# Decode scratch moved to PSUM, an order that knows the SBUF turn between VectorE and GpSimd, and first loads in another order

## The chip, the cores and the metric

The kernel runs on one core of a Trainium2 chip. The metric is the device time of one execution in microseconds (us). Five engines work side by side, each through its own instruction stream in order: TensorE (PE) multiplies into PSUM, ScalarE (ACT) and VectorE (DVE) compute on SBUF and PSUM, GpSimd (POOL) on SBUF, and SyncE (SP) issues most of the transfers.

## The reference

Attention over pooled keys, then a dense layer pair:

```python
k_p = k.reshape(B, H, Sp, 8, D).mean(axis=3)       # B=8, H=8, S=576, D=64, Sp=72
v_p = v.reshape(B, H, Sp, 8, D).mean(axis=3)
attn = softmax(q @ k_p.T / sqrt(D))                # 576 x 72 per head
x = (attn @ v_p) as 4608 x 512
h = x @ w_in                                       # 512 x 2048
out = (h * sigmoid(1.702 * h)) @ w_out             # 2048 x 512
```

`w_in` and `w_out` arrive as float64, so the kernel has to make fp32 numbers out of 64-bit words itself. All large products are done as three products of a high and a low part.

## The kernel before

Tokens go through the dense layers in nine chunks of 512: chunk c is 512 of the 576 tokens of batch c, the last chunk gathers the 64 left over of all eight. For each of 16 slices f of 128 hidden columns, PE makes h (L893 to L895), ACT makes the gelu twice, once rounded (gh, L908) and once in full (g, L914), DVE or POOL makes the low part gl = g - gh (L918), and PE adds gh and gl times w_out to o (L934 to L936). Chunk 0 is done in two halves of 256 tokens and pairs of slices, since it runs while the weights still arrive.

Attention of a batch: `sum_keys` and `sum_values` pool k and v (for batches 0 and 1 by matmuls against the identity, tiles red_k, red_v), `scores` makes sps on PE and on DVE nm (the row maximum) and sc, exp on ACT, the sum sm, its reciprocal, then tail and main (L582), and `weigh` turns these on PE (tpt, apt), splits them on ACT and DVE (at, ah, al) and multiplies by v (pav); ACT and DVE write the high and low half of x (L723, L729). Batch 0 has two pieces (256 and 320 tokens).

Weights: 33 pieces of 512 or 256 columns, in order w_in slice, w_out slice, and so on. `decode` takes for each: ACT writes e = |high word| scaled (L833), ACT scales the low word in place (L840), DVE shifts e (L846), DVE merges it with the sign into raw (L853), POOL adds the low word (L860), ACT rounds to the high part of w (L867), and POOL or DVE makes the low part (L873). The scratch e lies in SBUF, in a ring of two buffers ("osb") that only the output copies use later.

The order of all of this comes from `Plan`: each task has an engine, a cost, a due time, the tasks before it, and the buffers of limited rings that it takes. `order()` runs a clock over the five engines, gives each free engine the ready task with the earliest due time for which its rings have room, and the instructions are then written in the order found. PSUM has a ring "h" of two banks (dense h tiles, the key and value sums of batch 0), "a" of two and "o" of four. A DVE task costs 1.3 times as much in the plan while POOL is busy, a POOL task 1.2 times while DVE is.

Of the kernel before, what the change touches and what calls it, by code (L numbers as in the profile page):

```python
# [9 lines left out]
F32 = mybir.dt.float32  # L10
# [7 lines left out]
P = 128  # L18
POOL = 8

ENGINES = ("DMA", "ACT", "DVE", "POOL", "PE")

# [24 lines left out]
class Task:  # L47
    __slots__ = "engine us emit due after before bufs ready left begun table k".split()


class Plan:
# [6 lines left out]
    def add(self, engine, us, emit, reads=(), writes=(), due=None, table=None, also=()):  # L58
        t = Task()
        t.engine, t.us, t.emit, t.table = engine, us, emit, table  # L60
# [54 lines left out]
    def order(self, log=None):  # L115
        free = dict.fromkeys(ENGINES, 0.0)
        free["DMA"] = 2.0
        ready = {e: [] for e in ENGINES}
        for t in self.tasks:
            if not t.left:  # L120
                ready[t.engine].append(t)
        now, running, table, placed = 0.0, [], None, []
        busy = {}
        while len(placed) < len(self.tasks) or running:
            for end, k, t in sorted(running):
# [7 lines left out]
                for o in t.after:  # L133
                    o.left -= 1
                    o.ready = max(o.ready, end + self.wait(t, o))
                    if not o.left:
                        ready[o.engine].append(o)
            for e in ENGINES:
                if free[e] > now + 1e-9:
                    continue  # L140
                best = None
                for t in ready[e]:
                    if t.ready <= now + 1e-9 and (best is None or (t.due, t.k) < (best.due, best.k)) and self.room(t):
                        best = t
                if best is None:
                    continue
                t = best
                ready[e].remove(t)
                us = t.us
                if t.table not in (None, table):  # L150
# [18 lines left out]
            times += [t.ready for e in ENGINES for t in ready[e] if t.ready > now + 1e-9]  # L169
            if not times:  # L170
                if len(placed) < len(self.tasks):
                    stuck = [(t.engine, t.due, [b.name for b in t.bufs if b.ring is not None and not b.held and not b.ring.room]) for e in ENGINES[1:] for t in ready[e]] + [b.name for b in {b for t in placed for b in t.bufs if b.users and b.ring is not None}]
                    raise RuntimeError(f"stuck at {now}: {stuck}")
# [6 lines left out]
def attention_moe_kernel(ctx: ExitStack, tc: tile.TileContext, q, k, v, w_in, w_out, out):  # L180
# [53 lines left out]
    def dve(n, emit, reads, writes, rate=1.0, due=None, also=()):  # L234
        return plan.add("DVE", 0.14 + n / 960.0 * rate, emit, reads, writes, due, also=also)

    def pool(n, emit, reads, writes, rate=2.4, due=None):
        return plan.add("POOL", 0.06 + n * rate * 1e-3, emit, reads, writes, due)
# [95 lines left out]
    def spread(b, raw, bd, u, nm):  # L334
# [14 lines left out]
        else:  # L349
# [21 lines left out]
            [(bd, u)],  # L371
        )
# [4 lines left out]
    def sum_keys(b, m):  # L377
# [3 lines left out]
        for u in range(NU):  # L381
# [23 lines left out]
                [(m.tbd, u)],  # L405
            )
# [27 lines left out]
    def sum_values(b, m):  # L434
# [11 lines left out]
        def tsrc():  # L446
# [7 lines left out]
            [m.vl],  # L454
        )
# [7 lines left out]
            [m.vt],  # L463
        )
# [4 lines left out]
    def scores(b, piece, m, whole_q=None):  # L469
# [74 lines left out]
        for ns, g in groups:  # L544
# [26 lines left out]
            dve(200, inverse, [], [(sm, ns)])  # L571


        if b < TURNED:
            main = buf(att, [P, NT, H, KM], F32, "main", f"main{n}")
            tail = buf(att, [P, NT, H, KT], F32, "tail", f"tail{n}")
            for dst, cols in ((tail, slice(KM, KEYS)), (main, slice(0, KM))):
                for ns, g in groups:
# [10 lines left out]
                        [(dst, ns)],  # L589
                    )  # L590
# [3 lines left out]
        for i in range(4):  # L594
# [3 lines left out]
            for u in range(NU):  # L598
# [11 lines left out]
                    rate=1.8,  # L610
                )
            for r in range(4):
# [11 lines left out]
                    rate=1.25,  # L624
# [3 lines left out]
    def weigh(b, piece, m, main, tail):  # L628
# [29 lines left out]
        for u in range(NU):  # L658
# [16 lines left out]
            dve(npc, lo, [pt], [at])  # L675
# [3 lines left out]
        for j in range(NJ):  # L679
# [10 lines left out]
            else:  # L690
# [16 lines left out]
                [al],  # L707
            )
# [42 lines left out]
    def gather_left(c):  # L751
# [8 lines left out]
        for j in range(NJ):  # L760
# [12 lines left out]
                [(x, (1, 0, j))],  # L773
            )
# [36 lines left out]
    def decode(i):  # L811
# [4 lines left out]
        e = buf(moe, [P, DM], F32, "osb", f"e{i}")  # L816
# [7 lines left out]
        def eu():  # L824
# [24 lines left out]
            rate=0.5,  # L849
# [229 lines left out]
```

## Time and profile before

| what | value |
|---|---|
| median of 3 runs | 977.33 us (976.6 to 977.58) |
| the profiled execution | 976.99 us, its span 975.2 us |
| PE busy | 933.1 us (96%) |
| DVE, ACT, POOL busy | 551.7, 394.0, 246.7 us |
| mean granted clock of PE | 0.978 |

The span is the time from the first to the last instruction. PE is busy in 100 of 100 us between 200 and 300 us; the first 150 us, in which the weights arrive and are decoded and the first two batches go through attention, look different:

```profile
PE   5688899999999999999999999999999999999996
DVE  2899986688737793679457945794588210000000
PEclk8689999999999999999999999999999999999998
DMA  8982232330133012401240124002200020001001
```

Each digit is a slice of 24.4 us, in tenths; PEclk is the granted clock of PE.

### The profile page before, as it was taken

The numbers are of one execution on the slowest core, as the hardware profiler recorded it, in microseconds if no ns is written. First come the engines' busy times: TensorE is split into PE (matmuls) and PEld (weight loads), VectorE is DVE, ScalarE is ACT, GpSimd is POOL, SyncE is SP. The second block draws the span as 40 slices with busy tenths as digits, with TensorE's granted clock in tenths as the row PEclk, the third lists the DMA queues.
The fourth block names the chain that finished last, engine by engine and source line by source line (L and its number), as shares of the span: only waits on it lengthen the run. The fifth ranks groups of instructions, "written<-read, shape, count | busy, mean of one in ns | idle before, by whom it ended". The sixth has DMA issues, their size and how long they took to land.

```text
span 975.2 us, 12254 instructions
## 1 busy us (share of the span) xinstructions
PE 933.1 (96%) x4470; PEld 771.5 (79%) x4470; DVE 551.7 (57%) x1038; ACT 394.0 (40%) x745; POOL 246.7 (25%) x196
## 2 busy tenths in 40 slices
PE   5688899999999999999999999999999999999996
PEld 5467788888888888888888888888888878887884
DVE  2899986688737793679457945794588210000000
ACT  2777774444334432443244334343434231222112
POOL 1447841121222122212221221122221222222221
PEclk8689999999999999999999999999999999999998
DMA  8982232330133012401240124002200020001001
GB/s 199 348 300 50 54 61 71 92 75 12 36 79 81 12 30 68 99 12 25 68 104 11 28 65 103 11 23 71 70 1 1 6 87 1 1 0 44 1 1 43
DMA packets 104875, 59.52 MB, mean 61 GB/s; under 512 B 79472, under 2 KB 87664, under 8 KB 104688
## 3 DMA queue, kind: packets, MB, share of 16 engines
q1 hardware_dynamic: 99568, 49.31, 20.1%
q10 hardware_dynamic: 5248, 9.44, 2.8%
q8 instruction: 35, 0.57, 0.2%
q14 instruction: 24, 0.20, 0.1%
HBM read 48.23 MB, written 10.49 MB: 60 GB/s over the span
## 4 chain that ended last, share of the span: by engine, by line
PE 85%; DVE 6%; issue 2%; DMA 2%; ACT 2%; SPq 1%; ACTq 1%; POOL 0%; POOLq 0%; DVEq 0%
PE h L893 13%; PE o L934 13%; PE h L894 13%; PE h L895 13%; PE o L935 12%; PE o L936 12%; PE sps L509 4%; DVE raw L853 2%; DVE e L846 1%; PE pav L714 1%; PE pav L716 1%; PE pav L717 1%; PE pav L715 1%; DMA raw<-in_moe_w_in_dram 1%; SPq L289 1%
## 5 line engine op out<-in xcount | busy, mean ns | idle before, releaser
L918 POOL TENSOR_TENSOR gl<-g,gh 128x512 fp32r<-128x512 f32 x132 | 172.8, 1309 | 644.3 <-ACT g L914 522.3
L893 PE MATMUL h<-x,w 128*128 128x512 f32 (+1 forms) x640 | 241.9, 378 | 1.8 <-ACT g L914 1.8
L894 PE MATMUL h<-x,w 128*128 128x512 f32 (+1 forms) x640 | 237.2, 371 | 0.0
L895 PE MATMUL h<-x,w 128*128 128x512 f32 (+1 forms) x640 | 237.0, 370 | 0.0
L934 PE MATMUL o<-w,gh 128*128 128x512 f32 x576 | 229.4, 398 | 1.2 <-ACT gh L908 0.7
L936 PE MATMUL o<-w,gl 128*128 128x512 f32 x576 | 226.2, 393 | 2.5 <-DVE gl L918 1.4
L935 PE MATMUL o<-w,gh 128*128 128x512 f32 x576 | 227.3, 395 | 0.0
L908 ACT ACTIVATE gh<-h 128x512 fp32r<-128x512 f32 x144 | 86.1, 598 | 303.0 <-PE h L895 270.9
L893 PEld LDWEIGHTS h<-x,w 128*128 128x128 f32 x640 | 121.9, 190 | 24.3 <-ACT g L914 2.7
L895 PEld LDWEIGHTS h<-x,w 128*128 128x128 f32 x640 | 121.8, 190 | 20.5
L894 PEld LDWEIGHTS h<-x,w 128*128 128x128 f32 x640 | 122.0, 191 | 18.6
L936 PEld LDWEIGHTS o<-w,gl 128*128 128x128 f32 x576 | 108.5, 188 | 28.4 <-DVE gl L918 2.6
L934 PEld LDWEIGHTS o<-w,gh 128*128 128x128 f32 x576 | 108.5, 188 | 27.2 <-issue 2.4
L935 PEld LDWEIGHTS o<-w,gh 128*128 128x128 f32 x576 | 108.7, 189 | 20.6
L616 DVE TENSOR_TENSOR main<-sc,sm 32x256 f32<-32x256 f32 (+1 forms) x192 | 115.8, 603 | 2.8
L914 ACT ACTIVATE g<-h 128x512 f32<-128x512 f32 x144 | 85.4, 593 | 25.5 <-PE h L895 20.6
L498 DVE STREAM_TRANSPOSE qt<-qr 128x256 f32<-128x256 f32 (+1 forms) x56 | 25.8, 467 | 57.5 <-PE sps L509 55.8
L509 PE MATMUL sps<-k,qt 128*128 128x144 f32 (+1 forms) x320 | 55.5, 302 | 0.6 <-DVE at L667 0.6
L509 PEld LDWEIGHTS sps<-k,qt 128*128 128x128 f32 (+1 forms) x320 | 45.3, 185 | 10.4 <-issue 2.0
L860 POOL TENSOR_TENSOR raw<-raw 128x512 uint32<-128x512 uint32 x30 | 35.1, 1169 | 59.5 <-DVE raw L853 48.1
L723 ACT CAST x<-pav 128x256 fp32r<-128x256 f32 x64 | 23.7, 371 | 46.6 <-PE pav L717 45.6
L527 DVE TENSOR_REDUCE nm<-sps 128x4 f32<-128x288 f32 x96 | 37.1, 387 | 6.6 <-PE sps L509 6.4
(89 smaller groups left out, 878.1 us busy)
## 6 DMA issues: line engine op xcount, KB each, us to landing
out_dram<-osb ACTq DMA_DIRECT2D x32, 256.0 KB
raw<-in_moe_w_in_dram SPq DMA_DIRECT2D x15, 512.0 KB
raw<-in_moe_w_out_dram SPq DMA_DIRECT2D x15, 512.0 KB
kv_False<-in_k_dram SPq DMA_DIRECT2D x28, 256.0 KB
kv_True<-in_v_dram SPq DMA_DIRECT2D x28, 256.0 KB
qr<-in_q_dram SPq DMA_DIRECT2D x112, 40.0 KB
qr<-in_q_dram SPq DMA_DIRECT2D x112, 32.0 KB
tl<-in_v_dram SPq DMA_DIRECT2D x48, 64.0 KB
```

The costliest lines, as they stand in the source:

```text
L509: nc.tensor.matmul(ps()[:ns, t * PW : (t + 1) * PW], lhsT=qt()[:, s0 - o0 : s0 - o0 + ns], rhs=m.k2()[:, j], start=True, stop=True,)
L527: lambda ns=ns, g=g, hs=hs, view=view: nc.vector.tensor_reduce(out=nm()[:ns, g, hs], in_=view(), axis=AX.X, op=ALU.max, negate=True),
L616: lambda r=r, a=a, half=half, rows=rows, cols=cols, nt=nt: nc.vector.tensor_tensor(out=main()[32 * r : 32 * (r + 1), :, cols].rearrange("p ...
L893: nc.tensor.matmul(o, lhsT=w[:, 0, j], rhs=xs[:, 0, j], start=j == 0, stop=False)
L894: nc.tensor.matmul(o, lhsT=w[:, 1, j], rhs=xs[:, 0, j], start=False, stop=False)
L895: nc.tensor.matmul(o, lhsT=w[:, 0, j], rhs=xs[:, 1, j], start=False, stop=j == NJ - 1)
L908: lambda: nc.scalar.activation(out=gh(), in_=h(), func=AF.Gelu_apprx_sigmoid),
L914: 512, lambda: nc.scalar.activation(out=g(), in_=h(), func=AF.Gelu_apprx_sigmoid), [h], [g], table="gelu"
L918: engine.tensor_tensor(out=gl(), in0=g(), in1=gh().bitcast(F32), op=ALU.subtract)
L934: nc.tensor.matmul(o, lhsT=gh()[:, i, tok], rhs=w[:, 0], start=f == 0, stop=False)
L935: nc.tensor.matmul(o, lhsT=gh()[:, i, tok], rhs=w[:, 1], start=False, stop=False)
L936: nc.tensor.matmul(o, lhsT=gl()[:, i, tok], rhs=w[:, 0], start=False, stop=f == NF - 1)
```

## The change

Four things change. The scratch e of the decode goes from SBUF to a PSUM bank of the ring "h", the ring of two that the dense h tiles use too. The plan no longer stretches DVE and POOL tasks by factors: tasks marked `port` (all POOL tasks, and most DVE tasks whose operands all lie in SBUF) exclude one another, the later one waits in the plan until the other is through, and a marked DVE task ranks 20 us later while POOL holds the port; some planned rates change with it. The low parts of the weights, and of chunk 0's gl, are POOL tasks that DVE may take instead once their due time has passed; before, every fourth piece and the first slices were fixed to DVE. And the first loads come in another order.

```diff
     def order(self):
+        port = {"DVE": 0.0, "POOL": 0.0}
...
+                rival = {"DVE": "POOL", "POOL": "DVE"}.get(e)
+                blocked = rival is not None and port[rival] > now
                 best = None
                 for t in ready[e]:
-                    if t.ready <= now + 1e-9 and (best is None or (t.due, t.k) < (best.due, best.k)) and self.room(t):
-                        best = t
+                    if t.ready > now + 1e-9 or e != t.engine and now < t.due:
+                        continue
+                    rank = (t.due + (BLOCKED if blocked and t.port and e == "DVE" else 0.0), t.k)
+                    if (best is None or rank < best[0]) and self.room(t):
+                        best = rank, t
...
-                if e == "DVE" and free["POOL"] > now:
-                    us *= 1.3
-                if e == "POOL" and free["DVE"] > now:
-                    us *= 1.2
+                if t.port:
+                    if blocked:
+                        us += port[rival] - now
+                    port[e] = now + us
...
-        us = nbytes / 1e3 / (340.0 if run >= 1024 else 160.0 if run >= 256 else 90.0)
+        us = nbytes / 1e3 / (340.0 if run >= 1024 else 110.0 if run >= 256 else 80.0)
...
-        e = buf(moe, [P, DM], F32, "osb", f"e{i}")
+        e = buf(ps_h, [P, DM], F32, "h", f"e{i}")
...
             lambda: nc.vector.tensor_scalar(out=eu(), in0=eu(), scalar1=3, scalar2=None, op0=ALU.logical_shift_left),
             [],
             [e],
-            rate=0.5,
...
-        if i % 4 != 2:
-            pool(n, lambda: lower(nc.gpsimd), [(rb, rk), (h, (0, c0))], [(h, (1, c0))])
-        else:
-            dve(n, lambda: lower(nc.vector), [(rb, rk), (h, (0, c0))], [(h, (1, c0))])
+        pool(
+            n,
+            lambda: lower(nc.gpsimd),
+            [(rb, rk), (h, (0, c0))],
+            [(h, (1, c0))],
+            other=lambda: lower(nc.vector),
+        )
...
-        if c == 0 and fs[0] < 12:
-            dve(512, lambda: rest(nc.vector), [g, gh], [gl])
-        else:
-            pool(512, lambda: rest(nc.gpsimd), [g, gh], [gl])
+        pool(512, lambda: rest(nc.gpsimd), [g, gh], [gl], other=(lambda: rest(nc.vector)) if c == 0 else None)
...
-        for n, what in enumerate("w k0 k1 tk tv q q v0 v1 w w w w w q w q w q".split()):
+        for n, what in enumerate("k0 k1 tk q q v0 v1 tv w w w w w q q q w w".split()):
```

In the last line w is a weight piece, k and v the main parts of batch 0, tk and tv its last keys and values (tile tl), q a tile of 128 queries. The line numbers below differ between the two kernels; after, L863 is the old L833, L870 the old L840, L876 and L882 the old L846 and L853, L896 the old L867.

PE's stream at the start of the program, before (numbers behind the names are running counts; red_v sums values, kps turns the keys, sps are scores):

```order
L412 MATMUL kps_0_151<-ident,kbd_143 128x2x64 x2
L415 MATMUL kps_0_151<-ident,tbd_145 128x4x8
L486 MATMUL qps_0_0_160<-ident,q_0_126 128x128 x2
L486 MATMUL qps_0_1_164<-ident,q_0_126 128x128 x2
L412 MATMUL kps_1_169<-ident,kbd_143 128x2x64 x2
L415 MATMUL kps_1_169<-ident,tbd_145 128x4x8
L344 MATMUL red_v_180<-kv_97,ident 128x128 x8
L509 MATMUL sps_0_0_194<-k_167,qt_0_0_176 128x144 x2
L509 MATMUL sps_0_1_201<-k_167,qt_0_1_178 128x144 x2
```

and the same place after:

```order
L511 MATMUL qps_0_0_130<-ident,q_0_103 128x128 x2
L511 MATMUL qps_0_1_134<-ident,q_0_103 128x128 x2
L435 MATMUL kps_0_159<-ident,kbd_124 128x2x64 x2
L438 MATMUL kps_0_159<-ident,tbd_153 128x4x8
L435 MATMUL kps_1_172<-ident,kbd_124 128x2x64 x2
L438 MATMUL kps_1_172<-ident,tbd_153 128x4x8
L534 MATMUL sps_0_0_178<-k_166,qt_0_0_137 128x144 x2
L534 MATMUL sps_0_1_185<-k_166,qt_0_1_140 128x144 x2
L511 MATMUL qps_0_2_192<-ident,q_0_103 128x128 x2
L511 MATMUL qps_0_3_198<-ident,q_0_103 128x128 x2
L365 MATMUL red_v_203<-kv_95,ident 128x128 x8
```

The scores now stand ahead of the first value sum, and the key turns behind the query turns.

ACT's stream at the start, after (raw_147 is the first weight piece, e_163 its scratch, k_166 the scaled keys that sps reads; before, the first e stood at the head of the stream and its piece was the first load):

```order
L518 COPY qt_0_0_137<-qps_0_0_130 128x256
L518 COPY qt_0_1_140<-qps_0_1_134 128x256
L863 ACTIVATE e_163<-raw_147 128x512
L447 ACTIVATE k_166<-kps_0_159 128x288
L870 ACTIVATE raw_147<-raw_147 128x512
L480 CAST vt_176<-tbd_153 96x512
L447 ACTIVATE k_166<-kps_1_172 128x288
```

The copy of the keys now stands behind the first decode step, which waits for the ninth of the loads.

ACT's stream in the middle of chunk 0's first slices, after (gh and g read the h tiles h_0_4 and h_256_0):

```order
L870 ACTIVATE raw_337<-raw_337 128x512
L728 CAST ah_1_2_690<-apt_1_2_675 128x320
L728 CAST ah_1_3_693<-apt_1_3_680 128x320
L896 CAST w_5_701<-raw_315 128x512
L896 CAST w_5_723<-raw_337 128x512
L752 CAST x_378<-pav_1_2_717 128x256
L767 COPY left_1_661<-pav_1_2_717 128x64
L752 CAST x_378<-pav_1_3_725 128x256
L767 COPY left_1_661<-pav_1_3_725 128x64
L940 ACTIVATE gh_0_4_753<-h_0_4_625 128x512
L946 ACTIVATE g_0_4_758<-h_0_4_625 128x512
L863 ACTIVATE e_766<-raw_357 128x512
```

Between raw_337 and raw_357 no piece is decoded, since both banks of the ring "h" hold h tiles; before, decode steps stood through this stretch.

## Rows read from the trace of the kernel before

**Rows 1.** The page: busy time of PE; the costliest ACT group of the dense layers.
```profile
PE 933.1 (96%) x4470; PEld 771.5 (79%) x4470; DVE 551.7 (57%) x1038; ACT 394.0 (40%) x745; POOL 246.7 (25%) x196
...
L908 ACT ACTIVATE gh<-h 128x512 fp32r<-128x512 f32 x144 | 86.1, 598 | 303.0 <-PE h L895 270.9
```

**Rows 2.** Windows: from:to, length, busy us of each engine, then clock, DMA share, GB/s.
```profile
64.00:68.00 4.00, 4.00 (x18) 3.28 (x17) 3.92 (x7) 3.40 (x8) 1.42 (x1) 0.51 1.04 367
118.00:130.00 12.00, 11.35 (x71) 10.66 (x72) 11.83 (x18) 9.12 (x16) 9.47 (x7) 0.86 0.25 58
200.00:300.00 100.00, 100.00 (x465) 82.25 (x465) 67.78 (x136) 41.15 (x77) 21.53 (x16) 1.00 0.22 52
```

**Rows 3.** PE's waits from 58 to 152 us: total us, times, longest.
```profile
PE tpt L639 <- DVE tail L582: 4.4, 1, 4.4
PE kps L412 <- DVE kbd L364: 3.0, 1, 3.0
PE o L936 <- DVE gl L918: 1.4, 1, 1.4
PE red_v L344 <- DMA kv_True<-in_v_dram: 1.1, 1, 1.1
PE apt L639 <- DVE al L703: 1.0, 1, 1.0
```

**Rows 4.** DVE's groups from 60 to 145 us: busy us, mean ns.
```profile
L853 DVE SCALAR_TENSOR_TENSOR raw<-raw,e 128x512 uint32<-128x512 uint32 x21 | 23.3, 1110 | 0.4
L846 DVE TENSOR_SCALAR e<-e 128x512 uint32<-128x512 uint32 x22 | 19.2, 873 | 0.0
...
L703 DVE TENSOR_TENSOR al<-apt,ah 128x320 fp32r<-128x320 f32 x4 | 1.9, 483 | 0.0
```

**Rows 5.** DVE's timeline near 109 us: start, us, instruction.
```profile
108.83 0.41 DVE L364 TENSOR_TENSOR kbd<-red_k,mask 128x256 f32<-128x256 f32 x1
109.16 1.21 DVE L398 TENSOR_TENSOR tbd<-tred,mask 128x256 f32<-128x256 f32 x1
110.30 0.68 DVE L853 SCALAR_TENSOR_TENSOR raw<-raw,e 128x512 uint32<-128x512 uint32 x1
```

**Rows 6.** POOL's timeline at the same time.
```profile
108.58 1.50 POOL L873 TENSOR_TENSOR w<-raw,w 128x512 fp32r<-128x512 f32 x1
```

**Rows 7.** SP's timeline: the issues of the first and second weight piece.
```profile
0.74 0.46 SPq L804 DMA_DIRECT2D raw<-in_moe_w_in_dram  x1
...
16.77 0.59 SPq L804 DMA_DIRECT2D raw<-in_moe_w_out_dram  x1
```

**Rows 8.** ACT's timeline: the first step of the same two pieces.
```profile
4.94 0.66 ACT L833 ACTIVATE e<-raw 128x512 f32<-128x512 f32 x1 [2.93 <-DMA raw<-in_moe_w_in_dram]
...
23.81 0.69 ACT L833 ACTIVATE e<-raw 128x512 f32<-128x512 f32 x1 [4.21 <-DMA raw<-in_moe_w_out_dram]
```

**Rows 9.** PE's timeline: first value sum and first scores.
```profile
20.01 3.71 PE L344 MATMUL red_v<-kv,ident 128*128 128x128 f32 x16 [0.86 <-PE kps L415]
23.55 1.15 PE L509 MATMUL sps<-k,qt 128*128 128x144 f32 x8
```

**Rows 10.** DVE's timeline: decode steps ahead of tail and main, both pieces of batch 0.
```profile
32.01 0.68 DVE L873 TENSOR_TENSOR w<-raw,w 128x512 fp32r<-128x512 f32 x1
32.61 0.68 DVE L853 SCALAR_TENSOR_TENSOR raw<-raw,e 128x512 uint32<-128x512 uint32 x1
33.21 0.41 DVE L846 TENSOR_SCALAR e<-e 128x512 uint32<-128x512 uint32 x1
33.66 1.41 DVE L853 SCALAR_TENSOR_TENSOR raw<-raw,e 128x512 uint32<-128x512 uint32 x1
...
53.06 0.68 DVE L853 SCALAR_TENSOR_TENSOR raw<-raw,e 128x512 uint32<-128x512 uint32 x1
...
54.12 1.42 DVE L853 SCALAR_TENSOR_TENSOR raw<-raw,e 128x512 uint32<-128x512 uint32 x1
...
56.85 0.68 DVE L873 TENSOR_TENSOR w<-raw,w 128x512 fp32r<-128x512 f32 x1
...
57.91 0.69 DVE L853 SCALAR_TENSOR_TENSOR raw<-raw,e 128x512 uint32<-128x512 uint32 x1
```

More of the change, by code (lines that the diff above doesn't have):

```diff
@@ L21 @@
 ENGINES = ("DMA", "ACT", "DVE", "POOL", "PE")
+BLOCKED = 20.0
 class Ring:
@@ L47 @@
 class Task:
-    __slots__ = "engine us emit due after before bufs ready left begun table k".split()
+    __slots__ = "engine us emit due after before bufs ready left begun table k port other".split()
 class Plan:
@@ L113, in room, with order, offer @@
         return all(r.room >= n for r, n in need.items())
-    def order(self, log=None):
+    def order(self):
         free = dict.fromkeys(ENGINES, 0.0)
         free["DMA"] = 2.0
+        port = {"DVE": 0.0, "POOL": 0.0}
         ready = {e: [] for e in ENGINES}
+        def offer(t):
+            ready[t.engine].append(t)
+            if t.other is not None:
+                ready[t.other[0]].append(t)
         for t in self.tasks:
             if not t.left:
-                ready[t.engine].append(t)
+                offer(t)
         now, running, table, placed = 0.0, [], None, []
-        busy = {}
         while len(placed) < len(self.tasks) or running:
@@ L169, in order @@
             times += [t.ready for e in ENGINES for t in ready[e] if t.ready > now + 1e-9]
+            times += [t.due for e in ENGINES for t in ready[e] if t.other is not None and t.due > now + 1e-9]
             if not times:
                 if len(placed) < len(self.tasks):
-                    stuck = [(t.engine, t.due, [b.name for b in t.bufs if b.ring is not None and not b.held and not b.ring.room]) for e in ENGINES[1:] for t in ready[e]] + [b.name for b in {b for t in placed for b in t.bufs if b.users and b.ring is not None}]
-                    raise RuntimeError(f"stuck at {now}: {stuck}")
+                    raise RuntimeError(f"stuck at {now}")
                 break
@@ L232, in act, with dve, pool @@
         return plan.add("ACT", 0.17 + n * 0.85e-3, emit, reads, writes, due, table)
[L234 to L238, printed above, removed]
+    def dve(n, emit, reads, writes, rate=1.0, due=None, also=(), port=False):
+        return plan.add("DVE", 0.14 + n / 960.0 * rate, emit, reads, writes, due, also=also, port=port)
+    def pool(n, emit, reads, writes, rate=2.4, due=None, other=None):
+        if other is not None:
+            other = ("DVE", 0.14 + n / 960.0, other)
+        return plan.add("POOL", 0.06 + n * rate * 1e-3, emit, reads, writes, due, port=True, other=other)
     def pe(ns, emit, reads, writes, due=None, also=()):
@@ L454, in sum_values @@
             [m.vl],
+            port=True,
         )
@@ L463, in sum_values @@
             [m.vt],
+            port=True,
         )
@@ L609, in scores @@
                     [(tail, (i, u))],
-                    rate=1.8,
+                    rate=1.15,
+                    port=True,
                 )
@@ L623, in scores @@
                     [(main, (i, r))],
-                    rate=1.25,
+                    rate=1.03,
+                    port=True,
                 )
@@ L968, in first_batch @@
         m.tl = [Part(tl, u, lambda t, u=u: t[:, u]) for u in range(NU)]
-        whole, place = [], None
+        whole = []
         tiles = PIECES[0][1] + PIECES[1][1]
```

24 lines of the change are left out of this document (17 added, 7 removed).

## The prediction

> **What bounds the kernel now.** I read the page first. PE is busy 933.1 of 975.2 us [rows 1], so 42 us are all that the other engines can give back, beside time lost to a low clock. The view by windows then says where they lie: from 200 to 300 us PE is busy for 100.00 of 100.00 us at full clock [rows 2], and nothing that DVE or POOL do there can move the end. What is left is the start, the middle of the load phase, and a tail that the change does not touch. The list of PE's waits names the middle: between 58 and 152 us PE waits 4.4 us for tail, 3.0 for kbd, 1.4 for gl and 1.0 for al, all made by DVE, and 1.1 for a transfer [rows 3]. In the same stretch DVE has hardly a gap (11.83 of 12.00 us from 118 to 130) and POOL, with 9.47, has some [rows 2]. So until about 145 us DVE is the bound, and PE runs behind it with few gaps because it has other work queued. The end moves by the PE gaps that close and the half-clock stretches that go, and by no more, however much DVE saves.
>
> Why DVE is slow there is in the timeline. At 109 us POOL is in a 1.50 us subtraction [rows 6]. DVE's kbd, whose first operand lies in PSUM, takes 0.41 us beside it; tbd, the same shape with both operands in SBUF, takes 1.21 us, and ends when POOL does; the L853 behind it takes 0.68 us [rows 5]. Averaged from 60 to 145 us, L853 takes 1.110 us and L846 0.873 us [rows 4], against 0.68 and 0.41 undisturbed [rows 5, 10].
>
> **The decode steps.** With e in PSUM, L853 reads one SBUF and one PSUM operand, as kbd does, so I take 0.68 us: 21 x (1.110 - 0.68) = 9.0 us less. L846 reads and writes PSUM. No row shows DVE writing PSUM. From below the bound is its own 0.41 us; from above its present mean, 0.873. I take 0.68: kbd's 256 columns take 0.41 and al's 320 columns 0.483, both out of PSUM, 0.07 us for 64 columns, which makes about 0.68 for 512 [rows 4, 5]. So 22 x (0.873 - 0.68) = 4.2 us less. Together 13 of DVE's 85 us from 60 to 145 us (9 to 19 by the bounds).
>
> The row at 0.41 us is 512 columns in less time than kbd's 256, so L846 now runs at about twice the rate [rows 5, 10]. The Trainium skill, page "VectorE: DVE Perf Modes", section "Mode 2×_2P — use both read ports for one tensor", explains that: a single-source fp32 operation uses both read ports, and only if its data lie in SBUF, since PSUM has one. By that rule the change gives up the double rate, an undisturbed L846 gets 0.27 us slower, and this speaks against the change. The rule and the slope out of PSUM agree on the value taken; what it costs, 22 x 0.27 = 5.9 us, is already inside the 4.2 us that remain.
>
> ACT's two steps and POOL's two stay, and POOL loses fewer turns. More low parts of gl go to POOL in the new order, and fewer to DVE. POOL has about a fifth of the stretch free [rows 2], so I count this as nothing for PE; if that room were gone, gl would come late, at the price of the 1.4 us wait that exists today [rows 3].
>
> **The start.** The first weight piece is no longer the first load. In its place k comes first, but kps needs tbd, and tbd needs all of tl, whose v rows (tv) are now last before the weights. And ACT's copy of the keys stands behind e_163, which waits for the first weight piece; behind that ACT instruction stand the keys, vt and with them every score. Before, the second piece was issued at 16.77 us [rows 7]; after, the first stands in that place less one issue of 0.46, at 16.3. From issue to use took 4.2 us for the first piece and 7.0 for the second [rows 7, 8], so it is used between 20.5 and 23.3 us; I take 21 us, since less is queued ahead of it than at 16.77 us before. With 0.69 for e and as much again for the copy and its handovers, the first scores run at 22.4 us, where they ran at 23.55 [rows 9]. This gain goes again: red_v, 3.71 us [rows 9], stood ahead of the first scores and stands now between the first and the last. I count the start as 0 (between 1 us earlier and 2.5 us later).
>
> **Softmax of batch 0.** Ahead of the first tail DVE has a low part and three decode steps in a row, 0.68 + 0.68 + 0.41 + 1.41 = 3.2 us [rows 10]. After, three steps stand ahead of sm and one behind it, some 2.7 us, and vl is moved behind main: 1 us gained. Ahead of the second tail the rows hold three L853 and a low part, 0.68 + 1.42 + 0.69 + 0.68 = 3.5 us, and two L846 of 0.41 between them, together 4.3 us [rows 10]. After, one pair (1.4 us) is left there, and one pair more than now stands before the last halves of x. That makes 1.5 us gained. So the second tail comes about 2.5 us earlier (-2 to 5). The wait for it, 4.4 us [rows 3], shrinks but stays, as PE's 48 products run out before tail in the new order too.
>
> **The middle.** The waits for kbd, gl and al are 5.4 us [rows 3]. With 13 us taken off DVE I expect 4 of them to go (0 to 5.4); what is late next is the 1.1 us transfer, which stays. The granted clock was 0.51 from 64 to 68 us, after the 4.4 us wait, with PE busy throughout [rows 2]: the lower level, 1.2 GHz, and about 2 us lost. It follows a wait that stays, so I count nothing. From 118 to 130 us, after the 3.0 us wait for kbd, the mean was 0.86 over 11.35 busy us [rows 2], 1.6 us lost; I take 1 back (0 to 1.6).
>
> **The ring of two.** This is what the change adds. An h tile of chunk 0 holds its bank for 24 matmuls of 256 columns, at 465 of 512 columns in 100 us [rows 2] some 2.6 us, and two gelus of 0.598 [rows 1]: about 4 us, for 16 tiles 64 us. A scratch holds one for ACT's 0.69 and DVE's 0.68 + 0.68, with handovers 2.3 us and with DVE's queue perhaps 3.3: for 24 pieces 55 to 79 us. That is 119 to 143 of the 170 bank-us that two banks have in 85 us. Where an h tile waits for a bank, PE stands with all that is behind it (the o products and the turns of batch 1). Where e waits, ACT stands with the casts of w and the gelus behind it, and PE waits for those; the stretch without e in the new order, behind raw_337, is such a place. From below this costs 0; from above, if all 16 h tiles wait for the two DVE steps and a handover of a scratch, 16 x 1.6 = 26 us. I take 2.5 us, one or two such waits: the order of tasks counts the banks and puts o products in between.
>
> **Sum.** 976.99 us for the profiled execution, less 2.5 (second tail), less 4 (waits on DVE), less 1 (clock), plus 2.5 (ring): 972.0 us. The median of the runs is 0.34 us above the profiled execution, so the forecast is **972.3 us**.
>
> **Rivals.** (a) *Nearly all comes back*: no ring wait, the tail 5 us earlier, 5.4 us of waits and 3.6 us of clock gone, both low stretches: 977.3 - 14.0 = 963.3. For it speaks DVE's 13 us, against it that kbd and gl were late in a stretch in which PE was otherwise full, and that a wait for the tail remains. (b) *Nothing moves*: PE's gaps only change place, since an order packed by estimates leaves some other tile late; 977 us, within 2 us. For it: DVE stays near its limit, as attention of batch 2 moves into the time gained. (c) *The ring decides, slower*: 8 of 16 h tiles wait 1.6 us for a scratch, 12.8 us, against the 7.5 us gained: 977.3 - 7.5 + 12.8 = 982.6. It beats the gain from five such waits on. For it speaks the occupation of 70 to 84%, against it that e is short and PE often has o products to do; it would be seen between 60 and 150 us. (d) *PSUM frees nothing*: L846 and L853 stay as long beside POOL as now, L846 with 0.27 us more on each of 22; 5.9 us more for DVE, about 979. Against it stands kbd's 0.41 us beside POOL. (e) *A late start*: the first piece used at 23.3 us, the scores 1.4 us later, the clock low for longer: 2 to 3 us, which leaves 974 to 975 with the rest as forecast.
>
> The Trainium skill, "SBUF — State Buffer", section "Who interferes with whom", has the shared ports as a lock that one of the two engines holds for a whole instruction, taken by a VectorE operation with two SBUF inputs or at the double rate, and not by one with at most one SBUF input. The trace agrees with it in tbd's 1.21 and kbd's 0.41 us [rows 5]; by that rule (d) is out, and the chance that I leave it covers what no row shows, a DVE write to PSUM.
>
> **Chances.** The forecast, 968 to 975.3 us with (e): 0.49. (a), below 968: 0.14. (b): 0.17. (c): 0.15. (d): 0.05. Less than 0.2% (2 us) is what a measurement of this kernel can't tell from no change. Faster takes the forecast and (a), 0.63; same takes (b), 0.17; slower takes (c) and (d), 0.20. The range that leaves out 2 in 10 goes from 965.5, in the upper part of (a), to 979.5, which takes in (b) and the milder half of (c) and (d); the forecast's own is 968 to 975.3.
>
> **What would show it.** L876 at about 0.68 us and L882 at 0.68 us whatever POOL does: the decode steps are right. First scores near 22.4 us, the second tpt near 61 us: the start is right. PE's waits for kbd, gl and al gone between 64 and 150 us, and clock 1.0 from 118 to 130: the middle is right. Waits of PE for L882 or for g ahead of an h tile, or of ACT for L882 ahead of e, of more than 3 us in total: the ring costs more than I took. The forecast is wrong if the saving of DVE shows as idle DVE time while PE's gaps stay, or if PE has new gaps behind 150 us.

## The result and the profile after

| what | before | after |
|---|---|---|
| median of 4 runs | 977.46 us (976.6 to 977.63) | 969.42 us (967.22 to 969.63) |
| ratio, 95% interval | | 0.9914 (0.9897 to 0.9932) |
| profiled execution, its span | 976.99, 975.2 us | 967.22, 965.4 us |
| PE busy | 933.1 us | 928.7 us |
| span without PE busy | 42.1 us | 36.7 us |

The changed kernel is 8.0 us faster; 5.0 were forecast. Its profiled execution is the fastest of its runs, 2.2 us below their median, so the two traces differ by more, 9.8 us: 5.4 us of PE's gaps and 4.4 us of its busy time.

Where along the run the gain lies is read from one instruction that both kernels have, the first copy of chunk 1's output on ACT. It starts at 288.58 us before and at 279.65 after, 8.9 of the 9.8 us. Where the early gain was made shows in the waits. PE's waits in the first 150 us, before and then after (total us, times, longest):

```profile
PE qps L486 <- DMA q<-in_q_dram: 9.5, 5, 2.8
PE red_k L344 <- DMA kv<-in_k_dram: 7.3, 1, 7.3
PE tpt L639 <- DVE tail L582: 6.3, 2, 4.4
PE kps L412 <- DVE kbd L364: 3.1, 2, 3.0
...
PE red_v L344 <- PE kps L415: 0.9, 1, 0.9
```

```profile
PE kps L438 <- DVE tbd L420: 8.9, 2, 6.9
PE red_k L365 <- DMA kv<-in_k_dram: 5.7, 1, 5.7
PE h L925 <- DVE raw L882: 3.5, 4, 1.2
PE red_v L365 <- DVE raw L882: 2.7, 1, 2.7
PE tpt L667 <- DVE tail L607: 2.5, 3, 1.0
PE qps L511 <- DMA q<-in_q_dram: 1.2, 1, 1.2
```

The waits for kbd, gl and al [rows 3] are gone and the waits for tail are 3.8 us shorter. New are the two rows that name L882: there PE wants a bank of the ring "h" that a scratch still holds, 6.2 us in all.

At the start the waits for q are nearly gone and one for tbd is new. That moved PE's idle time and saved none of it: ahead of the first scores PE stood 10.8 us before and 16.0 after, between them and the first tpt 8.9 and 3.7, so 19.8 us in both. Three of the five waits for q lay behind the first scores, as PE's timeline before shows:

```profile
30.72 0.45 PE L486 MATMUL qps<-ident,q 128*128 128x128 f32 x1 [2.81 <-DMA q<-in_q_dram]
33.32 0.48 PE L486 MATMUL qps<-ident,q 128*128 128x128 f32 x1 [2.16 <-DMA q<-in_q_dram]
35.88 1.28 PE L486 MATMUL qps<-ident,q 64*128 64x64 f32 x4 [2.08 <-DMA q<-in_q_dram]
39.04 0.61 PE L639 MATMUL tpt<-ident,tail 128*64 128x128 f32 x2 [1.88 <-DVE tail L582]
```

PE's clock, by windows (from:to, length, busy us of each engine, then clock, DMA share, GB/s), before and after; the row from 118 to 130 us stands beside [rows 2]:

```profile
16.00:60.00 44.00, 31.52 (x169) 25.73 (x169) 33.84 (x66) 27.30 (x53) 13.97 (x13) 0.69 1.07 338
60.00:68.00 8.00, 4.41 (x18) 3.46 (x19) 7.82 (x14) 6.47 (x13) 3.73 (x3) 0.57 1.06 370
116.00:124.00 8.00, 5.35 (x31) 5.17 (x32) 7.90 (x9) 5.29 (x10) 7.31 (x6) 0.79 0.44 99
```

```profile
16.00:60.00 44.00, 30.87 (x168) 25.20 (x168) 36.13 (x71) 28.86 (x55) 19.65 (x17) 0.73 1.02 334
60.00:68.00 8.00, 7.26 (x27) 5.13 (x28) 7.81 (x13) 6.26 (x13) 5.21 (x4) 0.79 1.06 371
116.00:124.00 8.00, 7.72 (x47) 6.49 (x45) 7.13 (x14) 7.04 (x11) 4.93 (x5) 1.00 0.57 111
...
118.00:130.00 12.00, 11.02 (x74) 9.57 (x72) 10.90 (x17) 8.05 (x12) 5.36 (x6) 1.00 0.50 111
```

The clock of a window is a mean over all of it, idle time included. So what a low clock cost PE is added up from windows of 0.5 us, in each the busy time times the share of the clock that is missing. Before it comes to 9.3 us from 16 to 60 us, 2.2 from 60 to 68 and 1.7 from 116 to 124, together 13.2; after to 8.3, 1.7 and 0, together 10.1. So 3.1 of the 4.4 us of busy time came back through the clock, 1.7 of it in the stretch from 116 to 124 us; the other 1.3 I can't place (ends of matmuls are modelled).

From 60 to 145 us DVE's busy time fell from 81.89 to 68.89 us. The decode steps after, on DVE from 60 to 145 us, answer to [rows 4] (busy us, mean ns):

```profile
L876 DVE TENSOR_SCALAR e<-e 128x512 uint32<-128x512 uint32 x23 | 15.8, 689 | 3.0 <-ACT e L863 2.9
L882 DVE SCALAR_TENSOR_TENSOR raw<-raw,e 128x512 uint32<-128x512 uint32 x22 | 15.1, 688 | 0.7
```

And the start, SP, ACT and PE, which answers to [rows 7 to 9] (start, us, instruction, wait before it):

```profile
15.89 0.37 SPq L834 DMA_DIRECT2D raw<-in_moe_w_in_dram  x1
...
23.17 0.63 ACT L863 ACTIVATE e<-raw 128x512 f32<-128x512 f32 x1 [9.20 <-DMA raw<-in_moe_w_in_dram]
...
24.18 2.29 PE L534 MATMUL sps<-k,qt 128*128 128x144 f32 x8 [0.30 <-ACT k L447]
...
38.17 0.61 PE L667 MATMUL tpt<-ident,tail 128*64 128x128 f32 x2 [0.98 <-DVE tail L607]
...
59.50 0.41 PE L667 MATMUL tpt<-ident,tail 128*64 128x128 f32 x2 [0.75 <-DVE tail L607]
60.71 0.24 PE L667 MATMUL tpt<-ident,tail 64*64 64x64 f32 x1 [0.80 <-DVE tail L607]
```

The first weight piece is used at 23.17 us and the first scores run at 24.18, later than before (23.55). Still the first tpt stands at 38.17, where it stood at 39.04, and that of the second piece at 59.50, where it stood at 63.59. So of the 9.8 us 0.9 are gained up to the first tail, 3.2 between the two tails, 4.8 from there to the first copy of chunk 1's output, and 0.9 behind it.

### The profile page after: what moved, and what is told of

Read it like the earlier page. It is cut to its first block, busy times and chain, and to the rows that moved or that the text cites. A ratio compares the mean times of both kernels' runs of the same rounds, so it can differ in the third digit from the quotient of the medians.

```text
span 965.4 us, 12236 instructions
## 1 busy us (share of the span) xinstructions
PE 928.7 (96%) x4470; PEld 768.6 (80%) x4470; DVE 535.0 (55%) x1031; ACT 392.6 (41%) x745; POOL 250.7 (26%) x203
## 4 chain that ended last, share of the span: by engine, by line
PE 87%; DMA 3%; SPq 3%; DVE 2%; ACT 2%; issue 1%; ACTq 1%; POOL 0%; POOLq 0%; DVEq 0%
PE h L925 13%; PE o L963 13%; PE o L964 13%; PE h L926 13%; PE h L927 13%; PE o L965 13%; PE sps L534 4%; DMA raw<-in_moe_w_in_dram 2%; SPq L834 1%; SPq L1007 1%; PE pav L743 1%; SPq L310 1%; PE pav L745 1%; PE pav L744 1%; PE pav L746 1%
## 5 line engine op out<-in xcount | busy, mean ns | idle before, releaser
L950 POOL TENSOR_TENSOR gl<-g,gh 128x512 fp32r<-128x512 f32 x136 | 177.5, 1305 | 637.1 <-ACT g L946 584.1
L925 PEld LDWEIGHTS h<-x,w 128*128 128x128 f32 x640 | 120.4, 188 | 28.8 <-DVE raw L882 3.4
L927 PEld LDWEIGHTS h<-x,w 128*128 128x128 f32 x640 | 120.4, 188 | 20.4
L926 PEld LDWEIGHTS h<-x,w 128*128 128x128 f32 x640 | 120.5, 188 | 18.9
L643 DVE TENSOR_TENSOR main<-sc,sm 32x256 f32<-32x256 f32 (+1 forms) x192 | 123.5, 643 | 2.8
L731 DVE TENSOR_TENSOR al<-mt,ah 128x256 fp32r<-128x256 f32 (+1 forms) x48 | 32.5, 677 | 16.3 <-ACT ah L728 16.3
```

What stands on the lines that cost most here:

```text
L643: lambda r=r, a=a, half=half, rows=rows, cols=cols, nt=nt: nc.vector.tensor_tensor(out=main()[32 * r : 32 * (r + 1), :, cols].rearrange("p ...
L925: nc.tensor.matmul(o, lhsT=w[:, 0, j], rhs=xs[:, 0, j], start=j == 0, stop=False)
L926: nc.tensor.matmul(o, lhsT=w[:, 1, j], rhs=xs[:, 0, j], start=False, stop=False)
L927: nc.tensor.matmul(o, lhsT=w[:, 0, j], rhs=xs[:, 1, j], start=False, stop=j == NJ - 1)
L950: engine.tensor_tensor(out=gl(), in0=g(), in1=gh().bitcast(F32), op=ALU.subtract)
```

## The experiments

All times are medians, all ratios are to the kernel before on the same chip, with 95% intervals; the runs of before beside them scatter from 974.4 to 978.5 us. A kernel whose tasks changed was planned anew; where the order was held, this is said.

### The scratch alone: `e1_psum_only`

The kernel before with e's place changed, and the plan's rate for the shift with it, as in the change.

```diff
-        e = buf(moe, [P, DM], F32, "osb", f"e{i}")
+        e = buf(ps_h, [P, DM], F32, "h", f"e{i}")
...
-            rate=0.5,
```

> The kernel before with one edit: the decode scratch e lies in PSUM, in the ring of the h tiles; the order is made anew by the old rules. Theory A (the scratch's place frees DVE, and this is most of the gain): L846 near 0.69 us and L853 near 0.69 us from 60 to 145 us instead of 0.87 and 1.11, and the time 970 to 974 us, half or more of the 8 us gained. Rival B (the new order brings the gain, the place alone brings little or loses to the ring): 976 to 980 us, with the shorter DVE instructions followed by DVE gaps. Rival C (the first loads bring it): 976 to 978 us.

Measured: 978.77 us, 1.0023 (1.0014 to 1.0033): 2 us slower. The two decode steps took 0.69 us each, as in the changed kernel. DVE gained (65.75 us busy from 60 to 145 us, 81.89 before), and PE did not: its waits from 0 to 150 us show the ring instead.

```profile
PE h L892 <- DVE raw L852: 7.7, 5, 3.4
...
PE red_v L344 <- DVE raw L852: 3.2, 1, 3.2
```

That is 10.9 us of waits for a bank, against 6.2 in the changed kernel. It speaks for the rival in which the ring decides; but the order was made anew too, so this alone doesn't say what the place is worth.

### The same order, scratch in SBUF: `e2_sbuf_same_order`

The changed kernel, each engine's stream in the same order, but e's tile lies in the SBUF ring of before. The plan still counts a bank of "h" for it, and so writes the same order.

```diff
-        return Buf(ring, lambda: pool.tile(shape, dtype, tag=tag, name=name, **kw), name)
+        at = moe if pool is ps_h and name[0] == "e" else pool
+        return Buf(ring, lambda: at.tile(shape, dtype, tag="osb" if at is moe and pool is ps_h else tag, name=name, **kw), name)
```

> The changed kernel with the same instructions in the same order on every engine, but e in two SBUF buffers of the old ring; nothing waits for a bank of the ring h on account of e. Theory A: L876 and L882 stretch again to 0.85 and 1.1 us where POOL is busy, some 12 us more DVE time from 60 to 145 us, PE's waits for DVE come back, and the time is 973 to 978 us. Rival B: the order already keeps the two engines apart, the stretch is small (under 5 us), and the time is 968 to 971 us. Rival D (the ring costs as much as the place gains): PE's 3.5 us of waits for L882 and the 2.7 us of red_v go, and the time is 965 to 968 us.

Measured: 977.46 us, 1.0008 (1.0000 to 1.0017). So new order, loads and engine choice together, without the place, gain nothing, and the place in that order is worth all 8.0 us. That order was planned for e in PSUM, though, with its banks and its prices; an order that the new rules plan for e in SBUF was not run, and might do better than this one. The decode steps are back at 0.83 and 1.12 us. PE's waits from 0 to 150 us:

```profile
PE tpt L668 <- DVE tail L608: 10.9, 2, 7.4
PE kps L439 <- DVE tbd L421: 9.4, 2, 7.4
...
PE o L966 <- DVE gl L951: 3.7, 1, 3.7
...
PE o L966 <- POOL gl L951: 1.3, 1, 1.3
```

No wait names L883, as e holds no bank of the ring. Against the changed kernel the waits for tail are 8.4 us longer and those for gl 5.0 us; less the 6.2 us of ring waits, that is 7.2. The rest of the 11.3 us between the gaps of the two profiles (48.0 and 36.7) is in smaller rows. How the tail comes late is seen in DVE's timeline ahead of it, here with e in SBUF and below it the same instructions in the changed kernel:

```profile
34.62 0.41 DVE L877 TENSOR_SCALAR e<-e 128x512 uint32<-128x512 uint32 x1
35.07 1.41 DVE L883 SCALAR_TENSOR_TENSOR raw<-raw,e 128x512 uint32<-128x512 uint32 x1
...
38.00 1.19 DVE L877 TENSOR_SCALAR e<-e 128x512 uint32<-128x512 uint32 x1
39.12 1.26 DVE L592 TENSOR_SCALAR sm<-sm 128x16 f32<-128x16 f32 x1
...
40.70 0.29 DVE L608 TENSOR_TENSOR tail<-sc,sm 128x128 f32<-128x128 f32 x1
```

```profile
32.77 0.69 DVE L876 TENSOR_SCALAR e<-e 128x512 uint32<-128x512 uint32 x1
33.50 0.69 DVE L882 SCALAR_TENSOR_TENSOR raw<-raw,e 128x512 uint32<-128x512 uint32 x1
...
35.93 0.69 DVE L876 TENSOR_SCALAR e<-e 128x512 uint32<-128x512 uint32 x1
36.52 0.17 DVE L591 TENSOR_SCALAR sm<-sm 128x16 f32<-128x16 f32 x1
...
37.01 1.01 DVE L607 TENSOR_TENSOR tail<-sc,sm 128x128 f32<-128x128 f32 x1
```

With e in SBUF the shift takes 0.41 us where it doesn't wait for its turn and 1.19 where it does; in PSUM 0.69 each time. And the scratch isn't all that is hit: sm over 16 columns took 1.26 us in place of 0.17, and ended as POOL ended the two low parts that it was in. POOL's timeline of the kernel with e in SBUF:

```profile
37.62 2.73 POOL L903 TENSOR_TENSOR w<-raw,w 128x512 fp32r<-128x512 f32 x2
```

37.62 + 2.73 = 40.35, and 39.12 + 1.26 = 40.38. The small steps are not spared in the changed kernel either: there it is tail that meets a low part on POOL and takes 1.01 us, where it takes 0.29 with e in SBUF. From the first of these rows to the end of tail it is 6.4 us with e in SBUF and 5.3 in PSUM, and the first row itself stands 1.9 us earlier in PSUM.

### The old first loads: `e3_old_loads`

The changed kernel with the loads of before.

```diff
-        for n, what in enumerate("k0 k1 tk q q v0 v1 tv w w w w w q q q w w".split()):
+        for n, what in enumerate("w k0 k1 tk tv q q v0 v1 w w w w w q w q w q".split()):
```

> The changed kernel with the first loads in the order of before (a weight piece first, tv ahead of q, the late q tiles between weight pieces), the order made anew. Theory A: the first loads bring nothing net, 968 to 971 us. Rival C: the new loads are what brings the second tail forward by 4 us, and the time is 972 to 975 us. The tbd that the keys wait for should come at 14 to 17 us instead of 20 to 23 us, so the first scores should run before 24 us.

Measured: 977.46 us, 1.0006 (0.9995 to 1.0017), with runs from 974.2 to 979.3. The start is not where this was lost: the second tpt stands at 59.08 us and the first h tile of 512 columns of chunk 1 at 176.72 (177.96 in the changed kernel). From there on it falls behind, and the first output copy of chunk 1 comes at 282.88 (279.65). PE's waits from 150 to 700 us, where the changed kernel has none:

```profile
PE h L925 <- ACT g L946: 3.0, 5, 0.9
PE o L963 <- ACT osb L975: 2.3, 2, 2.1
PE pav L746 <- DVE al L731: 1.0, 1, 1.0
```

None of these rows names one of the first loads, and up to 150 us PE had been busy for 126.3 us, 2.8 more than in the changed kernel. So the likely cause is the new plan, which put other work late; a run with the old loads in a held order, which would show it, was not made. The time lies above both ranges expected. Hence the later experiments on what a plan made anew does by itself.

### The old rules of the plan: `e6_old_rules`

The changed kernel, planned by the factors 1.3 and 1.2 and the old rates, without the exclusion.

```diff
-                if t.port:
-                    if blocked:
-                        us += port[rival] - now
-                    port[e] = now + us
+                if e == "DVE" and free["POOL"] > now:
+                    us *= 1.3
+                if e == "POOL" and free["DVE"] > now:
+                    us *= 1.2
...
-        us = nbytes / 1e3 / (340.0 if run >= 1024 else 110.0 if run >= 256 else 80.0)
+        us = nbytes / 1e3 / (340.0 if run >= 1024 else 160.0 if run >= 256 else 90.0)
```

> The changed kernel with the plan's contention rules of before (factors 1.3 and 1.2, no exclusion, the old rates), while scratch, first loads and free choice of engine stay as changed. Theory A: the place of the scratch does the work and the rules little, 969 to 973 us. Rival B: without the rules DVE and POOL collide on the subtractions that still share SBUF (low parts, gl, tbd, vt), the DVE time from 60 to 145 us rises by 4 us or more, and the time is 974 to 978 us.

Measured: 970.45 us, 0.9934 (0.9918 to 0.9950). The intervals of this and of the changed kernel overlap: 0.2% lies between the two ratios, so the rules are worth some 1 to 2 us here, and may be worth nothing.

### Engines fixed as before: `e5_fixed_engines`

The changed kernel, the low parts bound to the engines of before (every fourth piece, and gl of the first slices, to DVE).

```diff
-        pool(
-            n,
-            lambda: lower(nc.gpsimd),
...
-            other=lambda: lower(nc.vector),
-        )
+        if i % 4 != 2:
+            pool(n, lambda: lower(nc.gpsimd), [(rb, rk), (h, (0, c0))], [(h, (1, c0))])
+        else:
+            dve(n, lambda: lower(nc.vector), [(rb, rk), (h, (0, c0))], [(h, (1, c0))], port=True)
```

> The changed kernel with the low parts fixed to their engines as before (every fourth weight piece and chunk 0's first gl on DVE), everything else as changed, the order made anew. The run with the scratch alone lost 3.4 us to 7.7 us of waits of PE's h products for the ring; the run with the old contention rules did not. Theory E (the free choice of engine keeps DVE early enough that the ring's banks come free): PE's waits for L882 grow to 6 us or more, and the time is 973 to 978 us. Rival F (the free choice matters little, the place and the loads do it): waits for L882 near 3.5 us, 968 to 971 us.

Measured: 987.26 us, 1.0105 (1.0088 to 1.0122), 18 us above the changed kernel. The time lies above both ranges expected. PE waits 5.8 us for g ahead of h, and 4.4 us for osb, the latter behind 150 us, as in the run with the old loads. Taken by itself this would make the free choice the heart of the change. The run with the order held, below, takes that back.

### One number of the plan by one: `e10_due_plus_1`

The changed kernel with the due times of all dense work 1 us later. Nothing that an engine executes changes but its order.

```diff
-    FIRST, STEP, ROUND = 44.0, 6.0, 96.0
+    FIRST, STEP, ROUND = 45.0, 6.0, 96.0
```

> The changed kernel with the due times of all dense work 1 us later (FIRST 45 instead of 44) and nothing else; the order is made anew. It measures how much a mere reshuffle of the order is worth. Theory G (the run with the old loads lost its gain to a reshuffle far behind the loads): the time differs from 969.4 us by 3 us or more, with waits behind 150 us. Rival H (the order is stable, and the old loads themselves cost 8 us): 968.5 to 970.5 us.

Measured: 972.91 us, 0.9959 (0.9947 to 0.9972): 3.5 us slower than the changed kernel. Its waits to 150 us are those of the changed kernel (9.4 us for tbd in place of 8.9, 3.5 for h on the ring and 2.5 for tail in both); between 150 and 300 us it has 2.1 us of gaps, and PE there waits 1.5 us for g.

### The same in the old kernel: `e11_before_due_plus_1`

The kernel before, with the same edit.

```diff
-    FIRST, STEP, ROUND = 44.0, 6.0, 96.0
+    FIRST, STEP, ROUND = 45.0, 6.0, 96.0
```

> The kernel before with the due times of all dense work 1 us later and nothing else; it measures what a reshuffle is worth in the old kernel. If the order of before is typical for its rules, 975 to 979 us; if it is a lucky one, 979 to 984 us, and then the run with the scratch alone (978.8 us) would be no loss; if an unlucky one, below 974 us.

Measured: 988.55 us, 1.0127 (1.0113 to 1.0140): 12.2 us slower, for due times that moved by 1 us, and above all three ranges expected. PE's waits over the whole run:

```profile
PE o L934 <- ACT osb L946: 4.2, 5, 2.6
PE o L936 <- DVE gl L918: 3.4, 5, 1.4
```

The first of these comes to 0.4 us in the kernel before, the second is 2.0 us longer than there [rows 3]. So a comparison of two kernels planned apart can carry 3.5 or 12 us, as in these two, that belong to no edit, and the order of before may be a lucky one.

### The same order, engines fixed: `e13_same_order_fixed`

The order of the changed kernel held task for task, but each low part written to the engine of the old rule: 20 on DVE in place of 13.

```diff
+        who = nc.vector if i % 4 == 2 else nc.gpsimd
...
-            lambda: lower(nc.gpsimd),
+            lambda: lower(who),
...
-            other=lambda: lower(nc.vector),
+            other=lambda: lower(who),
```

and the same with gl of chunk 0.

> The changed kernel's order word for word, but each low part is done on the engine that the old rule fixes (every fourth weight piece and chunk 0's first gl on DVE, 20 in all, where the changed kernel has 13 there). Theory E (who does the low parts matters by itself): waits of PE for gl and for L882 grow, and the time is 973 to 980 us. Rival G (the 10 us lost in the run with fixed engines came from the reshuffle, not from the engines): 969 to 972 us.

Measured: 969.42 us, 0.9933 (0.9920 to 0.9947), the changed kernel's median to the last digit. The choice of engine is worth nothing that shows; the 18 us of the kernel with fixed engines came with its new plan.

### Old rules and old loads: `e12_old_rules_old_loads`

The changed kernel with the old rules and rates and the old loads, that is the kernel before with the scratch in PSUM and the free choice of engine.

```diff
-                if t.port:
...
+                if e == "DVE" and free["POOL"] > now:
+                    us *= 1.3
...
-        for n, what in enumerate("k0 k1 tk q q v0 v1 tv w w w w w q q q w w".split()):
+        for n, what in enumerate("w k0 k1 tk tv q q v0 v1 w w w w w q w q w q".split()):
```

> The kernel before with two parts of the change, the scratch in PSUM and the free choice of engine for the low parts, but with the old contention rules and the old first loads. Theory E (the free choice is what the scratch alone lacked): PE's waits for the ring drop from 10.9 us in the run with the scratch alone to under 7, and the time is 969 to 973 us. Rival C (the first loads are needed): 976 to 980 us.

Measured: 975.94 us, 0.9992 (0.9981 to 1.0002), with runs from 973.1 to 977.4. Ring waits of PE are 6.0 us (3.9 for h, 2.1 for red_v), and PE waits 3.2 us for g and 1.5 for al behind 150 us. The ring's waits fell as theory E had it, the time did not. Inconclusive: the difference to the changed kernel, 6.5 us, is within what a new plan does.

### The value sums out of the ring: `e8_sums_in_o`

The changed kernel; the key and value sums of batch 0 take banks of the ring "o" of four.

```diff
-            red = buf(ps_h if b == 0 else ps_a, [P, 512], F32, "h" if b == 0 else "a", f"red{b}_{nm}")
+            red = buf(ps_o if b == 0 else ps_a, [P, 512], F32, "o" if b == 0 else "a", f"red{b}_{nm}")
```

> The changed kernel with the key and value sums of batch 0 in the ring o of four PSUM banks (idle at the start) instead of the ring h, the order made anew. Theory: the second value sum no longer waits 2.7 us for a scratch, tail of the second piece comes 1 to 2 us earlier, and the time is 967.5 to 969 us. Rival: the wait is hidden behind the softmax of the first piece, which ends later than the value sum, and the time is the same as of the changed kernel, 969 to 971 us.

Measured: 968.87 us, 0.9911 (0.9895 to 0.9928), equal to the changed kernel. The 2.7 us that red_v waited for a bank are gone, and the waits for tail are 9.0 us in place of 2.5. In this new plan the ring wait taken away at the start has turned into a wait for the softmax, so that nothing shows of the 2.7 us at the end.

### The last values loaded earlier: `e7_tv_early`

The wait for tbd, 8.9 us, is the longest of the changed kernel. tbd needs all of tl, whose rows tv are loaded last before the weights; here they are loaded right behind tk.

```diff
-        for n, what in enumerate("k0 k1 tk q q v0 v1 tv w w w w w q q q w w".split()):
+        for n, what in enumerate("k0 k1 tk tv q q v0 v1 w w w w w q q q w w".split()):
```

> The changed kernel with tv, the tail rows of v, ahead of q in the first loads (k0 k1 tk tv q q v0 v1 w ...), the order made anew. In the changed kernel the keys wait 8.9 us for tbd, which needs tv. Theory: the first scores run at 18 to 20 us instead of 24.2, the first tail 2 us or more earlier, and the time is 966 to 968.5 us. Rival: the softmax of the first piece then waits for something else (q, the value sums, the weights' decode), and what is gained is lost to the reshuffle, whose size the run with due times 1 us later gave as 3.5 us: 969 to 973 us.

Measured: **964.97 us** (964.28 to 966.29), 0.9887 (0.9873 to 0.9901). It is the best kernel of the study: none of its runs reaches the fastest of the changed kernel (967.22), and in one series it stood against 969.42 of the kernel with the same order and fixed engines. PE's timeline:

```profile
15.34 0.69 PE L435 MATMUL kps<-ident,kbd 128*128 128x128 f32 x2 [2.68 <-DVE kbd L385]
...
17.35 2.29 PE L534 MATMUL sps<-k,qt 128*128 128x144 f32 x8
...
31.54 0.41 PE L667 MATMUL tpt<-ident,tail 128*64 128x128 f32 x2 [4.32 <-DVE tail L607]
```

The scores run 6.8 us earlier and the first tpt 6.6 us earlier (38.17 in the changed kernel), the second tpt at 55.40. Scores and time come out better than the ranges expected. By the medians some 4.4 of the 6.8 us reach the end; the two profiled executions differ by 0.9 only, as one is the slowest of its four runs and the other the fastest. The plan was made anew here as well; that the wait went where the edit took it away speaks for the edit, but the 4.4 us lie within what a new plan can do.

### Sums out of the ring and the last values early: `e9_sums_in_o_tv_early`

The changed kernel with the two edits before this one.

```diff
+            red = buf(ps_o if b == 0 else ps_a, [P, 512], F32, "o" if b == 0 else "a", f"red{b}_{nm}")
...
+        for n, what in enumerate("k0 k1 tk tv q q v0 v1 w w w w w q q q w w".split()):
```

> Both edits together: value and key sums of batch 0 in the ring o, and tv ahead of q. Theory: 965 to 968 us, the best version. Rival: the waits for tail grow as in the run with the sums in o (9.0 us in two waits), and the time is 968 to 972 us.

Measured: 965.15 us, 0.9894 (0.9877 to 0.9911), equal to the one with tv early alone. The ring waits are 9.2 us here (5.4 for h, 3.8 ahead of qps).

## Why the prediction was right, and where its sizes were wrong

The direction and the mechanism were right: DVE was the bound of the early middle, and the scratch in PSUM took it off (shown by the kernel with the same order and e in SBUF). The sum came to 5.0 us between the two profiled executions, and 9.8 were measured. By its steps, from the rows of PE's waits and windows:

| step | taken | measured |
|---|---|---|
| wait for tail | -2.5 | -3.8 (6.3 to 2.5) |
| waits for kbd, gl, al | -4 | -5.5 (3.1 + 1.4 + 1.0, all gone) |
| clock, 116 to 124 us (taken for 118 to 130) | -1 | -1.7 |
| clock, up to 68 us | 0 | -1.4 |
| start, waits of PE | 0 | -1.9 (17.7 to 15.8) |
| ring of two | +2.5 | +6.2 |
| not placed (PE busy 1.3, small waits) | | -1.7 |

**Decode.** Right in size: 0.689 and 0.688 us against 0.68 for both. The slope over columns of other DVE instructions out of PSUM held for a write to PSUM too. The Trainium skill's page "VectorE: DVE Perf Modes", section "Mode 2×_2P — use both read ports for one tensor", gives the double rate only to data in SBUF; the undelayed shift at 0.41 us with e in SBUF and at 0.69 in PSUM agrees. The rival in which PSUM frees nothing is out, and DVE's 13 us came as forecast. One reading was not exact: tbd did not end when POOL did [rows 5, 6] but 0.29 us later (110.37 and 110.08 us), so an instruction that has to wait for its turn takes the rest of POOL's instruction and then some time of its own.

**The start.** This step failed in its parts, and its total came near the 0 that was taken by luck, as two errors cancelled. I took the first weight piece to be used at 21 us; it was 23.17, at the end of my bounds, and the first scores came at 24.18, not 22.4. I had seen that the keys need a late tbd, and put no price on it: it became the longest wait, 8.9 us. What I had not seen is that the waits for the queries behind the first scores, 7.0 us, would go. In the table that is 9.5 + 7.3 + 0.9 = 17.7 us for q, kv and kps before and 1.2 + 5.7 + 8.9 = 15.8 for q, kv and tbd after; the 1.9 us saved went, with 0.9 of the wait for the first tail, to the value sum's wait for a bank, and PE stood 19.8 us ahead of the first tail in both kernels. The clock lost 0.9 us less before 60 us. A late start I had priced at 2 to 3 us, by when its last instruction runs and not by how long PE stands until then; it came, and cost nothing that shows.

**Softmax of batch 0.** Right in kind, too small: the second tpt was expected near 61 us and stands at 59.50, with its last part at 60.71. The wait "shrinks but stays", from 4.4 to 1.5 us; the rest of the table's 3.8 is the first tail. I had counted nothing for the low clock behind it; that stretch stayed, and cost 0.5 us less.

**The middle.** Right: all of the DVE waits went, a little more than I took, and the clock was 1.00 from 118 to 130 us.

**The ring.** The step that was mis-sized most: 6.2 us of waits, 2.5 taken. I had set 3 us as the point from which it costs more than I took, and it is passed. I counted h tiles against scratches but not the value sum of batch 0, which takes a bank of the same ring and waited 2.7 us of the 6.2; the h tiles, which the sum was about, waited 3.5. A wait is not yet a cost: without the 2.7 us the kernel with the sums in the other ring was no faster. The kernel with the scratch alone, at 10.9 us of such waits and 2 us slower, suggests that the rival in which the ring decides was near, though those 2 us are less than a new plan moves.

**What stays open.** How much of the gain belongs to the loads: the kernels with the old loads were planned anew, and a new plan alone moved 3.5 and 12 us. All three with the scratch in PSUM and the old loads lie at 975.9 to 978.8 us, six of the seven plans with the scratch in PSUM and the new loads (tv early or late) at 965 to 973. So it is not excluded that the place needs the new loads to pay. In the one comparison with a held order the place carries all of it, and the loads, the rules and the choice of engine together, without the place, carry 0 to 1.7 us of loss. Whether the place would also pay in the old kernel's order, with no plan made anew, was not tried, nor what the new rules would plan for a scratch in SBUF.

## What to carry to other kernels

Where a planner writes the order, hold the order when you ask what an edit is worth, and move the due times by 1 us to learn how much a new plan moves by itself; here that was as large as the change. A PSUM operand takes a DVE instruction out of its turns with POOL (those beside it whose operands lie in SBUF keep theirs), but the bank is paid for by every user of its ring, so count them all, the short-lived ones at the start too. Price a start by how long the bound engine stands and at which clock, not by the time of one instruction.

## What was not expected of the hardware

A DVE instruction of 16 columns took 1.26 us beside POOL and 0.17 us elsewhere: what a turn costs is set by the rest of POOL's instruction, not by DVE's own size, so small steps of a softmax lose the most for their size. Five such steps, of 16 or 8 columns, took 1.06 to 1.26 us in the kernel before and the one with e in SBUF and the new order, and each ended about 0.03 us after a low part on POOL. Decode steps with a PSUM operand did not vary: 22 and 23 of them of 512 columns from 60 to 145 us at a mean of 0.69 us, each between 0.66 and 0.71, with POOL busy 62.18 of 94 us in much the same stretch (58 to 152 us). And kernels that do the same work in different orders scatter by different amounts, 2.4 us for the changed kernel (4 runs) and 5.1 for the one with the old loads (11 runs); part of that may be the number of runs, and the profile of one execution doesn't tell more.
